# Attention and gated feed-forward on one core: keys of twelve tiles projected in four column groups, weight loads held back at transpositions, head reordered

## The chip, the cores and the metric

The kernel runs on one core of a Trainium2 chip. The metric is the device time of one execution in microseconds (us). The engines in the text are TensorE (PE, matrix products; PEld is its weight load), VectorE (DVE), ScalarE (ACT), GpSimd (POOL) and SyncE (SP, which only issues DMAs here). The core's memory has 128 partitions; products land in PSUM banks of 128 x 512 float32 values.

## What is computed

One pre-norm transformer block on x of 2048 rows and 1024 columns in bf16. The first half is attention with 32 query heads of 32 columns that share one key head and one value head. The second half is a gated feed-forward (FFN) of width 3584.

```python
q = (x @ wq).reshape(B, S, H, Dh).transpose(0, 2, 1, 3)
k = x @ wk
v = x @ wv
scores = einsum("bhqd,bkd->bhqk", q, k) * Dh ** -0.5
o = einsum("bhqk,bkd->bhqd", softmax(scores), v)      # then back to (B, S, H * Dh) @ wo
h = x + A(layernorm(x))
h2 = h + (sigmoid(n @ w_gate) * (n @ w_up)) @ w_down  # n = layernorm(h)
```

## The kernel before

**Tiles.** The 2048 rows are 16 tiles of 128. Two neighbouring tiles form a unit of the FFN, so there are eight units. Attention of a tile runs as four groups of eight heads over half of the keys each; a group is eight "bursts". A burst (`s_burst`) is four products of 32 x 512, one in each row group of the array, and fills four PSUM banks with scores of one key tile. ACT takes them in two exponentials of 128 x 1024 (`one_exp`, line 768). There are 512 bursts. The keys therefore have to stand four times over the partitions (`kT4`): the array's row group j reads keys from partitions 32j to 32j+31.

**Head.** Up to about burst 64 ("the head") the kernel normalizes x tile by tile (`ln1_stats`, `ln1_sub`, `ln1_mult`), transposes each normalized tile into `xnT`, and projects keys, values and queries from it. Tiles 0 and 1 are transposed by PE through PSUM banks of `S_ps` (`pe_transpose`, `pe_out`), the others by a DMA transposition on SP's queue (`transposed`, line 564). The key weights of 32 columns are copied four times side by side (`wk4`, 128 columns), so that `k_group` gives the four copies in one product per 128 rows of the contraction: eight products of 128 columns for each key tile. `v_group` and `q_tile` / `q_group` project values and queries. The groups of the head wait in a list `todo`, whose order is the string list `TODO`; `head_group` takes the first of it that is ready.

**Products by columns.** After a product with scores (four row groups) a change to another shape of the array costs PE time. A product for the FFN or the projections can also be cut into four column groups of 32 (`mm`, line 344, four instructions) so that no change of shape stands between it and the products of probabilities and values (`pv_group`, line 855), which use column groups too.

**Sums of probabilities.** For most groups DVE adds the probabilities in pairs (lines 805 and 817) and PE multiplies one sum with ones (line 902). For the groups marked `p` in `SUM_PLAN` PE multiplies all eight bursts with ones itself (line 917).

**After attention of a tile.** The output projection (`wo_group`), the second normalization (`stats2`, on DVE and POOL), and a DMA transposition on SP's queue (`transpose2`, `QT<-hn`). Then the unit's gate and up products (weights in halves of 512 KB that SP loads as slots come free), and its down products (`down_group`), whose weights `wd` (14 loads of 512 KB, `load_wd`, on POOL's queue) go into the places that x and the query weights held and stay there. The first down product waits for all 14. When only the first tile of a unit is ready, its gate and up products are done alone (`first_tile`), the other's come later.

**Order.** All instructions are emitted by a planner: a loop at the end of the kernel keeps an estimated clock for each engine and each DMA (`k_pe`, `k_dma`, the costs `T_EXP` and others) and decides, burst by burst, which group PE takes next. Strings steer it: `PV_PLAN` has a letter for each group of probabilities times values, `WO_PLAN` for each unit's output projection. `urgent(c)` puts a unit's output projection and normalization ahead when the unit before it is nearly through. The order on the chip is then fixed; only waits can stretch it.

**Start.** SP issues the left half of x tile 0, tiles 1 to 3, then three of the four parts of wq; ACT's queue issues the right half of tile 0, wk, the first part of wq, and wv. The first burst needs the queries of heads of q blocks 0 to 3, which come from the first two parts of wq.

Of the kernel before, what the change touches and what calls it, by code (L numbers as in the profile page):

```python
# [12 lines left out]
P = 128  # L13
# [55 lines left out]
class _Group:  # L69


    def __init__(self, items, evac, after=(), kind="f"):
        self.items = collections.deque(items)
        self.evac = evac
        self.after = after
        self.bank = None
        self.kind = kind
        self.room = 0.5
        self.first = False
# [5 lines left out]
def bass_sequential_preLN__grouped_kv_mqa__glu_gated_glu__prompt_kernel(  # L85
# [70 lines left out]
    with ExitStack() as es:  # L156
# [99 lines left out]
        def _(unused):  # L256
            sp, pe, act, dve, pool = nc.sync, nc.tensor, nc.scalar, nc.vector, nc.gpsimd

            def dma(q, dst, src, c, kb=256):
# [3 lines left out]
                k_dma[0] = begin + kb / 275.0  # L263
                c.at[c.n] = k_dma[0] + 2.2
# [60 lines left out]
            I_US, I_MAX = 4.0, 240  # L325
# [112 lines left out]
            mean_val, xc_val = {}, {}  # L438
            LOADS = {2: (4, 5), 3: (6, 7), 4: (8, 9), 5: (10, 11), 6: (12,), 7: (13,), 8: (14,), 9: (15,)}

            def ln1_stats(t, parts=(0, 1)):
# [5 lines left out]
                if parts[-1] == 0:  # L447
                    return
                need(dve, c_dve.inc(ins))
# [52 lines left out]
            def pe_transpose(t):  # L502

                need(pe, xn_val[t], ident_val)
                for dt in range(DT):
                    ins = pe.matmul(S_ps[:, 2 * t + dt // 4, dt % 4 * P:(dt % 4 + 1) * P], lhsT=xn(t)[:, dt * P:(dt + 1) * P],
# [9 lines left out]
            def pe_out(eng, t, h0, h1, *ticks):  # L516
                need(eng, *ticks)
                dst = xnT_tile(t)[:, 4 * h0:4 * h1, :]
                src = S_ps[:, 2 * t + h0:2 * t + h1, :].rearrange("p a (b q) -> p (a b) q", q=P)
# [41 lines left out]
            def transposed(eng, dst, src, slot, *ticks):  # L561
# [7 lines left out]
                c.at[c.n] = max(clk[0], k_dma[0] if eng is sp else 0.0) + 2.0  # L569
# [1041 lines left out]
```

## Time and profile before

| | |
|---|---|
| median of 3 runs | 1100.51 us (1100.1 to 1102.04) |
| the profiled execution | 1100.78 us |
| its span, first to last instruction | 1099.0 us |
| DVE busy | 895.4 us (81%) |
| ACT busy | 1003.7 us (91%) |
| POOL busy | 63.8 us (6%) |
| mean granted clock of PE | 0.997 |

Times inside the profile run from the first instruction. A row of a timeline has the start, the length, the engine, the line of the kernel, the operation, what it writes and reads, the shape and how many instructions were merged; in brackets the time for which the engine stood idle before it, and what ended that. A product's recorded length holds its way through the array, so that neighbours overlap; the distance between starts is what it costs PE. A row of a table by stretches has the stretch, its length, the busy time of each engine with the number of instructions, the granted clock, the share of DMA time and GB/s.

### The profile page before, as it was taken

What the parts mean: (1) busy time and instruction counts of PE and PEld (TensorE: products, weight loads), DVE (VectorE), ACT (ScalarE), POOL (GpSimd) and SP (SyncE); (2) the same over time, 40 slices, a digit from 0 to 9 for tenths busy, and PEclk for the clock granted to TensorE, in tenths of its full rate; (3) what the DMA queues carried; (4) which work ended last, traced back from release to release, by engine and by line L of the source; (5) the groups of instructions that cost most, each with busy time, mean ns of one, the idle gap of its engine ahead of it and who ended that gap; (6) DMA issues with size and microseconds to landing.
All of it is one profiled execution on the core that took longest, in us unless ns stands there. A gap on an engine that the chain in (4) does not pass through costs nothing.

```text
span 1099.0 us, 34241 instructions
## 1 busy us (share of the span) xinstructions
PE 1070.7 (97%) x15024; PEld 618.1 (56%) x15076; DVE 895.4 (81%) x1485; ACT 1003.7 (91%) x1145; POOL 63.8 (6%) x136
## 2 busy tenths in 40 slices
PE   8999979999999999999999999999999999999999
PEld 7443346643666346653666446653666447653884
DVE  7969878798988989798988988989988888798311
ACT  7999979999999999999999999999999999998110
POOL 3420010100000000000000000000000000000000
PEclk9999999999999999999999999999999999999999
DMA  8673246960976539791876619671495619662660
GB/s 194 139 157 134 64 111 193 270 150 21 236 204 189 135 92 249 196 214 31 212 206 187 153 31 260 192 190 38 129 244 157 147 35 258 191 186 57 162 161 20
DMA packets 320229, 170.12 MB, mean 155 GB/s; under 512 B 39376, under 2 KB 314064, under 8 KB 320080
## 3 DMA queue, kind: packets, MB, share of 16 engines
q1 hardware_dynamic: 314272, 157.70, 56.6%
q0 software_dynamic: 2544, 9.44, 2.7%
q8 instruction: 119, 1.95, 0.8%
q10 hardware_dynamic: 3264, 0.79, 0.4%
q14 instruction: 30, 0.25, 0.1%
HBM read 155.84 MB, written 4.19 MB: 146 GB/s over the span
## 4 chain that ended last, share of the span: by engine, by line
PE 79%; ACT 10%; DMA 4%; DVE 3%; issue 3%; POOL 1%; SPq 0%; ACTq 0%; DVEq 0%
PE X_ps L342 43%; PE X_ps L344 14%; PE S_ps L748 12%; PE X_ps L855 9%; ACT Pr L768 8%; DMA QT<-hn 2%; DMA wgu<-in_B_w_up_dram 1%; DMA zone<-in_A_wq_dram 1%; ACT QT L768 1%; PE X_ps L902 1%; ACT wo L768 1%; PE X_ps L917 0%; DVE pairs L805 0%; DMA zone<-hn 0%; POOL sd L424 0%
## 5 line engine op out<-in xcount | busy, mean ns | idle before, releaser
L768 ACT ACTIVATE Pr<-S_ps 128x1024 bf16<-128x1024 f32 x992 | 943.6, 1188 | 9.4 <-PE S_ps L748 8.7
L805 DVE TENSOR_TENSOR pairs<-Pr 128x1024 bf16<-128x1024 bf16 x470 | 320.3, 683 | 27.5 <-ACT Pr L768 27.1
L817 DVE TENSOR_TENSOR pairs<-pairs 128x1024 bf16<-128x1024 bf16 x408 | 281.4, 690 | 11.8
L748 PE MATMUL S_ps<-QT,kT 32*128 32x512 bf16 x2048 | 202.2, 385 | 4.3 <-ACT Pr L768 2.9
L342 PE MATMUL X_ps<-QT,wgu 128*128 128x128 bf16 (+1 forms) x2073 | 197.0, 245 | 2.4 <-DMA QT<-hn 1.2
L342 PEld LDWEIGHTS X_ps<-QT,wgu 128*128 128x128 bf16 x2073 | 153.8, 98 | 37.9 <-issue 22.6
L342 PE MATMUL X_ps<-QT 128*128 128x128 bf16 (+1 forms) x1484 | 142.5, 245 | 0.1
L748 PEld LDWEIGHTS S_ps<-QT,kT 32*128 32x128 bf16 x2048 | 51.5, 91 | 160.3 <-ACT Pr L768 145.8
L342 PE MATMUL X_ps<-zone,hact 128*128 128x512 bf16 (+2 forms) x599 | 137.0, 370 | 4.6 <-issue 4.0
L1172 ACT ACTIVATE gu<-X_ps 128x512 f32<-128x512 f32 x112 | 86.5, 773 | 48.4 <-PE X_ps L342 48.3
L1194 DVE SCALAR_TENSOR_TENSOR hact<-gu,X_ps 128x512 bf16<-128x512 f32 x112 | 76.6, 684 | 63.4 <-PE X_ps L342 52.6
L855 PE MATMUL X_ps<-Pr,V 128*32 128x512 bf16 x1984 | 128.0, 381 | 0.3 <-issue 0.3
L342 PEld LDWEIGHTS X_ps<-QT 128*128 128x128 bf16 x1484 | 110.4, 98 | 23.8 <-issue 14.5
L342 PEld LDWEIGHTS X_ps<-zone,hact 128*128 128x128 bf16 x636 | 55.0, 98 | 68.4 <-issue 16.1
L855 PEld LDWEIGHTS X_ps<-Pr,V 128*32 128x32 bf16 x1984 | 46.7, 96 | 52.5 <-issue 15.2
L344 PE MATMUL X_ps<-zone,hact 128*32 128x512 bf16 x1152 | 72.3, 380 | 0.0
L344 PE MATMUL X_ps<-QT,wgu 128*32 128x256 bf16 (+1 forms) x2076 | 63.6, 264 | 0.0
L344 PEld LDWEIGHTS X_ps<-QT,wgu 128*32 128x32 bf16 x2076 | 48.8, 97 | 12.7 <-issue 7.7
L413 POOL CAST mean<-mv 128x1 f32<-128x1 bf16 x28 | 7.3, 260 | 836.3 <-DVE mv L1064 808.7
L342 PE MATMUL X_ps<-wo,QT 128*128 128x512 bf16 x191 | 48.4, 380 | 1.4 <-issue 1.0
L342 PE MATMUL X_ps<-zone 128*128 128x128 bf16 (+3 forms) x442 | 45.0, 250 | 0.6 <-DMA zone<-in_A_wq_dram 0.5
L344 PEld LDWEIGHTS X_ps<-zone,hact 128*32 128x32 bf16 x1152 | 28.8, 96 | 29.3 <-issue 5.9
(99 smaller groups left out, 653.7 us busy)
## 6 DMA issues: line engine op xcount, KB each, us to landing
wgu<-in_B_w_gate_dram SPq DMA_DIRECT2D x75, 512.0 KB, 5.6
wgu<-in_B_w_up_dram SPq DMA_DIRECT2D x74, 512.0 KB, 5.2
QT<-in_B_w_up_dram SPq DMA_DIRECT2D x49, 512.0 KB, 5.3
QT<-in_B_w_gate_dram SPq DMA_DIRECT2D x48, 512.0 KB, 5.5
zone<-in_B_w_down_dram POOLq DMA_DIRECT2D x14, 512.0 KB, 5.4
hx<-in_A_x_dram SPq DMA_DIRECT2D x17, 256.0 KB, 2.8
out_dram<-hx SPq DMA_DIRECT2D x31, 128.0 KB, 1.7
Pr<-in_B_w_gate_dram SPq DMA_DIRECT2D x5, 512.0 KB, 7.0
```

Source lines behind the costliest of these rows:

```text
L342: return pe.matmul(out, lhsT=lhsT, rhs=rhs, start=start, stop=stop, skip_group_check=main[0])
L344: ins = pe.matmul(out[DH * j:DH * (j + 1)], lhsT=lhsT[:, DH * j:DH * (j + 1)], rhs=rhs, start=start, stop=stop, tile_position=(0, DH * j), ...
L413: return c_pool.inc(pool.tensor_copy(out=mean[:, i:i + 1], in_=mv[:, i:i + 1, 0]), 0.2)
L748: ins = pe.matmul(S_ps[:, ((2 * k + j // 2) % 3) * 2 + j % 2, :], lhsT=kT4[DH * j:DH * (j + 1), kt * P:(kt + 1) * P], rhs=QT[DH * j:DH * ( ...
L768: c_e.inc(act.activation(out=p_tile(k, n % 2), in_=S_ps[:, 2 * pr:2 * pr + 2, :].rearrange("p a (b q) -> p (a b) q", q=QC), func=ACTF.Exp, ...
L805: slot_use[x] = c_dve.inc(dve.tensor_tensor(out=dst(x), in0=p_tile(k - 1, hh), in1=p_tile(k, hh), op=ALU.add), T_ADD, 0.08)
L817: slot_use[x] = slot_use[y] = c_dve.inc(dve.tensor_tensor(out=pairs[:, x, :], in0=pairs[:, x, :], in1=pairs[:, y, :], op=ALU.add), T_ADD, ...
L855: ins = pe.matmul(bank[DH * j:DH * (j + 1), :], lhsT=V[:, kt, :], rhs=p_tile(kx, j // 2)[:, j % 2 * 2:j % 2 * 2 + 2, :], start=b == bs[0], ...
L902: ins = pe.matmul(bank[DH * j:DH * (j + 1), :], lhsT=ones[:], rhs=pairs[:, sum_wide[(g, j // 2)], j % 2 * 512:(j % 2 + 1) * 512], start=Tr ...
L1172: tanh_val[n] = c_act.inc(act.activation(out=slot, in_=bank, func=ACTF.Tanh, scale=0.5), T_TANH, 0.1)
L1194: gu_read[n] = c_dve.inc(dve.scalar_tensor_tensor(out=hact[:, 2 * fs[0]:2 * fs[0] + ft, r0:r0 + len(ts) * P], in0=slot.rearrange("p (a b) ...
```

## The change

Keys of tiles 0 to 3 are projected as before. Keys of tiles 4 to 15 come in three groups of four tiles: `kc_group` (C1 to C3) projects a tile in each column group with the 32 columns of `wk`, DVE copies the result to a staging place, and `kr_group` multiplies it with columns of the unit matrix, which spreads each tile's keys over the four partition groups; DVE copies that to `kT4`. The staging place is the old place of `wk4`. A C group waits until four tiles of `xnT` are there.

`load_wd` isn't issued while `turning()` holds: from the time at which a tile's attention is normalized until its transposition has landed. The down loads begin at burst 50 in place of 10, and all of them wait for the exponentials of the burst before.

At the start the second part of wq is issued ahead of x tiles 2 and 3, and x tiles 4 and 5 follow the third and fourth part; the keys and the first two query pairs of tile 0 are projected ahead of the transposition of tile 1, which now uses other banks; the first burst waits for tile 0 alone. The list `TODO` has another order.

Some PSUM evictions of the queries move between ACT and DVE (`T_PLAN`, `Q_PLAN`), `SUM_PLAN` marks one group more (group 4) for PE, `urgent` goes by the work left (`U_PLAN`), and the planner's strings, thresholds and costs have new values.

```diff
+    ROOM = 0.5
...
-    NEAR = 2
-    PV_PLAN = "BDaeeaaaAbbaaBbaAEeAababaAbBeAaaEAAaeDbdeaAbbbaEDabAAabaAaaabaAaacbcabDa"
-    WO_PLAN = "bbabaaaa"
+    U_PLAN = "65531610"
+    PV_PLAN = "aeaadddabaadbababaBbEdaaAaBbebdaaCdDdacaabAAdaaBaaCdDacdaaaaccbaaBbBaaaE"
+    WO_PLAN = "abbabaaa"
-    BANK_WAIT = 0
+    BANK_WAIT = 0.05
-    SUM_PLAN = "ppppdddp"
+    LN_RATE = 0.3
+    T_PLAN = "aaadddad"
+    H_ROOM = 0.5
+    Q_PLAN = "daddddddddddddddddadddddddddaddd"
+    SUM_PLAN = "pppppddp"
-    TODO = ["k1", "k0", "q1a", "q1b", "q0a", "q0d", "q0c", "q0b", "k2", "q1d", "k5", "k4", "ka", "v1", "v0", "k7",
-            "q1c", "v3", "v2", "k3", "k6", "kc", "kf", "kd", "kb", "ke", "v4", "v7", "v5", "k8", "v6", "Q2",
-            "k9"]
+    TODO = ["v7", "q1a", "k2", "q1b", "C1", "v1", "q1c", "v5", "v4", "k1", "C2", "v3", "Q2", "q0c", "q0d", "v2",
+            "v6", "C3", "v0", "q1d", "k3"]
-    WD_FROM, WD_GAP, WD_LATE = 10, 4, 6
-    K_ACT = 2
-    T_MM, T_FIX, T_SW, T_EXP, T_TANH, T_ADD = 0.0004167, 0.00267, 0.104, 0.91, 0.48, 0.61
+    WD_FROM, WD_GAP, WD_LATE = 50, 4, 14
+    K_ACT = 0
+    T_MM, T_FIX, T_SW, T_EXP, T_TANH, T_ADD = 0.0004167, 0.00267, 0.1, 0.907, 0.479, 0.61
...
-            for t in range(1, 4):
-                load_x(t)
+            load_x(1)
             wk_val = dma(act, wkr, A_wk.rearrange("(a p) j -> p a j", p=P), d_w[0], 64)
             wq_val[0] = dma(act, wq[:, 0, :, :], wqr[:, :, 0:256], d_w[2], 512)
+            load_wq(1, 256, 256)
+            for t in range(2, 4):
+                load_x(t)
             wv_val = dma(act, wv, A_wv.rearrange("(a p) j -> p a j", p=P), d_w[1], 64)
-            for i in range(1, 4):
+            for i in range(2, 4):
                 load_wq(i, 256 * i, 256)
+                load_x(i + 2)
...
-            I_US, I_MAX = 4.0, 240
+            I_US, I_MAX = 4.0, 210
...
-            LOADS = {2: (4, 5), 3: (6, 7), 4: (8, 9), 5: (10, 11), 6: (12,), 7: (13,), 8: (14,), 9: (15,)}
+            LOADS = {2: (6, 7), 3: (8,), 4: (9, 10), 5: (11,), 6: (12,), 7: (13,), 8: (14,), 9: (15,)}
...
+            def kc_group(i):
+                tiles = range(4 * i, 4 * i + 4)
+                items = []
+                for dt in range(DT):
+                    def f(bank, dt=dt):
+                        for j, t in enumerate(tiles):
+                            ins = pe.matmul(bank[DH * j:DH * (j + 1), 0:P], lhsT=wkr[:, dt, :],
+                                            rhs=xnT[:, t // TPQ, dt, t % TPQ * P:(t % TPQ + 1) * P], start=dt == 0,
+                                            stop=dt == DT - 1, tile_position=(0, DH * j), skip_group_check=True)
+                        return mm_done(ins, 144, dt == DT - 1)
+                    items.append((0.06, f))
...
+                    need(dve, tick)
+                    stage_val[i] = c_dve.inc(dve.tensor_copy(out=stage(i), in_=bank[:, 0:P]), 0.25, 0.08)
+                    for t in tiles:
+                        xnT_done(t // TPQ, tick)
+                    todo.insert(0, ("r", i))
...
+            def kr_group(i):
+                c0, items = 4 * i * P, []
+                for j in range(4):
+                    def f(bank, j=j):
+                        for r in range(4):
+                            ins = pe.matmul(bank[DH * r:DH * (r + 1), j * P:(j + 1) * P], lhsT=stage(0)[:, DH * j:DH * (j + 1)],
+                                            rhs=stage(i), start=True, stop=True, tile_position=(0, DH * r),
+                                            skip_group_check=True)
+                        return mm_done(ins, 144, j == 3)
+                    items.append((0.06, f))
...
+                    v = c_dve.inc(dve.tensor_copy(out=kT4[:, c0:c0 + 4 * P], in_=bank), 0.65, 0.08)
...
-                need(pe, (c_e, 2 * k - 1) if k > 0 else None, *s_ready(k), *(xnT_ready(0, 1) if k < 2 else ()))
+                need(pe, (c_e, 2 * k - 1) if k > 0 else None, *s_ready(k), *(xnT_ready(*range(k + 1)) if k < 2 else ()))
...
-                return not q_list and downs <= NEAR and downs < len(ffn_list) and unit_of(ffn_list[downs]) == c
+                if q_list:
+                    return False
+                left = 0.0
+                for x in ffn_list:
+                    if unit_of(x) == c:
+                        return left <= 3.0 * int(U_PLAN[c])
+                    left += {"p": 7.0, "l": 3.5, "g": 1.75, "u": 1.75, "d": 6.0}[x[0][0]]
+                return False
...
             ln1_stats(0)
+            ln1_sub(0)
             ln1_stats(1)
-            ln1_sub(0)
+            ln1_mult(0)
+            ln1_stats(1, ())
             ln1_sub(1)
-            ln1_mult(0)
...
             f0, f1 = pe_transpose(0)
+            xnT_val[0] = [pe_out(act, 0, 0, 1, f0), pe_out(dve, 0, 1, 2, f1)]
             ln1_mult(1)
-            xnT_val[0] = [pe_out(act, 0, 0, 1, f0), pe_out(dve, 0, 1, 2, f1)]
+            run_group(k_group([0], True))
+            run_group(q_tile(0, [0, 1], True))
+            run_group(q_tile(0, [2, 3], True))
             f0, f1 = pe_transpose(1)
...
-                return len(xn_val) >= min(NT, (k[0] // 4 if k[0] < NHB else k[0] - NHB + BPG) + LN_LEAD)
+                return len(xn_val) >= min(NT, int(LN_LEAD + LN_RATE * k[0]))
...
+            def turning():
+                t = len(hnT_val)
+                return t < NT and (t, NQ // 2 - 1) in ot_val or t and when(hnT_val[t - 1]) > k_pe[0]
...
-                if wd_free and wo_val[0] and k[0] >= wd_at[0] and when(*wd_free[0][1]) <= k_pe[0]:
+                if wd_free and wo_val[0] and k[0] >= wd_at[0] and when(*wd_free[0][1]) <= k_pe[0] and not turning():
                     load_wd()
```

More of the change, by code (lines that the diff above doesn't have):

```diff
@@ L518, in pe_out @@
                 dst = xnT_tile(t)[:, 4 * h0:4 * h1, :]
[L519 removed]
+                src = S_ps[:, 4 * t + h0:4 * t + h1, :].rearrange("p a (b q) -> p (a b) q", q=P)
                 if eng is act:
@@ new lines, in kr_group, with evac @@
+            def kr_group(i):
[8 more added lines that the diff above has]
+                    items.append((0.06, f))
+                def evac(bank, tick):
+                    need(dve, tick)
+                    v = c_dve.inc(dve.tensor_copy(out=kT4[:, c0:c0 + 4 * P], in_=bank), 0.65, 0.08)
+                    for t in range(4 * i, 4 * i + 4):
+                        k_val[t] = v
+                        wk_done(tick)
+                    return v
+                return _Group(items, evac, [same_val[0], stage_val[i]], "pv")
@@ L1426, in head_group @@
                         ok = q_can(*x[1:], now)
+                    elif x[0] == "r":
+                        ok = when(stage_val[x[1]], same_val[0]) <= now
+                    elif x[0] == "C":
+                        tiles = range(4 * x[1], 4 * x[1] + 4)
+                        ok = len(k_val) >= 4 and all(t in xnT_val for t in tiles) and when(*xnT_ready(*tiles)) <= now
                     else:
@@ L1484, in _ @@
                 can_s = kk < NB and pv_done[0] >= ring_need(kk - 1 if late else kk) and (
-                    s_ready(kk) is not None and when(*s_ready(kk)) <= k_pe[0])
+                    kk >= NHB + 5 * BPG or s_ready(kk) is not None and when(*s_ready(kk)) <= k_pe[0])
                 hold = (busy(pv[0]) and plan_of(pv_next[0] - 1) in "deDE" and pe_mode[0] == "pv" and
```

56 lines of the change are left out of this document (39 added, 17 removed).

## The prediction

> **What bounds the kernel now.** I read the page first, then tables by stretches, the chain that ended last, and timelines of the places that these point to.
>
> ```profile
> span 1099.0 us, 34241 instructions
> PE 1070.7 (97%) x15024; PEld 618.1 (56%) x15076; DVE 895.4 (81%) x1485; ACT 1003.7 (91%) x1145; POOL 63.8 (6%) x136
> ACT  7999979999999999999999999999999999998110
> PE 79%; ACT 10%; DMA 4%; DVE 3%; issue 3%; POOL 1%; SPq 0%; ACTq 0%; DVEq 0%
> ```
>
> PE holds 79% of the chain. ACT is full until slice 37 and then nearly idle: the exponentials are over, and PE works off what is left.
>
> ```profile
> 30.00:60.00 30.00, 27.42 (x561) 13.96 (x561) 26.88 (x63) 30.00 (x34) 12.84 (x31) 1.00 0.63 123
> 140.00:160.00 20.00, 15.29 (x245) 9.27 (x242) 18.96 (x33) 18.07 (x21) 4.08 (x7) 0.99 0.51 120
> 160.00:180.00 20.00, 16.96 (x301) 12.35 (x302) 12.25 (x20) 14.98 (x18) 0.72 (x1) 0.84 0.49 125
> 800.00:900.00 100.00, 99.03 (x1296) 54.28 (x1296) 86.24 (x138) 100.00 (x116) 1.93 (x4) 1.00 0.58 148
> 900.00:1000.00 100.00, 98.53 (x1538) 60.00 (x1539) 87.15 (x142) 99.31 (x115) 3.51 (x7) 1.00 0.71 184
> ```
>
> In the table by stretches PE and ACT are both full from 800 to 1000 us. So the time is the sum of PE's work and of PE's gaps. A us less of either pulls the end forward by a us, as long as PE has products at hand. The large gap lies between 140 and 180 us: 7.7 us without PE work, and a granted clock of 0.84 in the second half.
>
> **Term 1: the down loads leave the transposition of tile 1.**
>
> ```profile
> 151.54 1.49 POOL L260 DMA_DIRECT2D zone<-in_B_w_down_dram  x2
> 152.19 1.24 SPq L564 DMA_TRANSPOSE QT<-hn  x1
> 162.41 1.36 PE L342 MATMUL X_ps<-QT,zone 128*128 128x128 bf16 x11 [6.64 <-DMA QT<-hn]
> 164.35 1.94 ACT L768 ACTIVATE Pr<-S_ps 128x1024 bf16<-128x1024 f32 x2 [6.28 <-PE S_ps L748]
> 162.00:166.00 4.00, 3.59 (x32) 2.96 (x33) 0.59 (x1) 1.65 (x2) 0.00 (x0) 0.50 0.00 0
> QT<-hn SPq DMA_TRANSPOSE x1, 10.2
> QT<-hn SPq DMA_TRANSPOSE x1, 4.4
> 131.84 1.24 SPq L564 DMA_TRANSPOSE QT<-hn  x1
> QT<-hn SPq DMA_TRANSPOSE x1, 6.7
> 236.45 4.08 SPq L564 DMA_TRANSPOSE QT<-hn  x1
> ```
>
> Two down loads of 512 KB are issued at 151.5 us, the transposition at 152.19, and it lands 10.2 us later. PE stands 6.64 us, and then works four us at half clock: 3.6 us of work at 0.50 lose 1.8 us. ACT stands 6.28 us of the same time. The transposition of tile 0 (131.84) took 4.4 us, that of tile 2 (236.45) took 6.7 us; no down load is issued beside either. The change forbids the loads from a tile's normalized attention to the landing. At 4.4 us the landing comes at 156.6 in place of 162.4: the gap shrinks by 5.8 us to 0.8, and the 1.8 us go too. That is 7.6 us. With 6.7 us the gap keeps 3.1 us; what the clock does after 3.1 us no row shows (the row shows it after 6.64), so the gain is 3.5 to 5.3 us. I take 7.6: as in the row of 4.4, SP has only loads of x close by. The upper bound is 8.4, the whole gap and its slow clock.
>
> The Trainium skill ("TensorE: Matmul & The Clock Gate", section "HAM oscillation — how this bites in real kernels") asks that PE have no idle gap above about 3.4 us, since one makes it start again at half clock. The trace agrees with its 6.64 us gap and the clock of 0.50. By that rule a gap of 3.1 us costs only itself, and the gain would be 5.3 us.
>
> **Term 2: keys in four column groups.**
>
> ```profile
> 45.34 0.63 PE L344 MATMUL X_ps<-zone 128*32 128x128 bf16 x32
> 45.78 0.40 PE L917 MATMUL X_ps<-Pr,ones 128*32 128x512 bf16 x4
> 134.84 1.48 PE L917 MATMUL X_ps<-Pr,ones 128*32 128x512 bf16 x24
> 67.22 4.89 DMA zone<-hn
> ```
>
> The row at 45.34 is one key tile by columns: eight sets of four products, and the next work starts 0.44 us later, 55 ns a set. Twelve tiles take 96 sets. The change takes 3 x 8 for the projection and 3 x 4 for the spreading, of the same shape: 36. Sixty sets less are 3.3 us. The four streams now read different rows; in the row at 134.84, where each set of four ones products reads four different slices of probabilities, a set costs (1.48 - 0.39) / 5 = 0.218 us for 512 columns, a fourth of which is again 55 ns.
>
> The same part marks group 4 for PE in the sums. It then takes eight sets with ones in place of one: seven more at 0.218 us are 1.5 us of PE. DVE loses eight adds and six merges at about 0.69 us, but DVE isn't the bound. Net, 1.8 us off PE. It counts while queries are still being projected when the FFN begins; they are:
>
> ```profile
> 138.32 0.82 PE L342 MATMUL X_ps<-zone 128*128 128x512 bf16 x3
> 138.98 0.94 PE L342 MATMUL X_ps<-QT,zone 128*128 128x128 bf16 x14
> ```
>
> The last query product ends and the first gate product starts without a gap, so what the head saves starts the FFN earlier. DVE's twelve key evictions become three small and three wide ones, which is free. The keys now come in batches: the batch of tiles 12 to 15 needs the transposition that lands at 67.22 + 4.89 = 72.1 us, then some 2 us of projecting, copying, spreading and copying. Burst 36 uses it first, at 12.5 + 36 x 1.83 = 78 us (both from term 3). Covered by 4 us; if normalization slips by more, every us of it stops ACT and PE alike.
>
> **Term 3: the start.**
>
> ```profile
> 2.97 8.91 DMA zone<-in_A_wq_dram
> 8.22 0.58 ACT L521 ACTIVATE zone<-S_ps 128x512 bf16<-128x512 f32 x1
> 9.13 0.68 DVE L522 CAST zone<-S_ps 128x512 bf16<-128x512 f32 x1
> 11.50 0.38 ACT L642 ACTIVATE QT<-X_ps 128x256 bf16<-128x256 f32 x1 [0.62 <-PE X_ps L342]
> 11.92 1.34 PEld L342 LDWEIGHTS X_ps<-zone 128*128 128x128 bf16 x24 [0.64 <-DMA zone<-in_A_wq_dram]
> 13.63 0.39 PE L748 MATMUL S_ps<-QT,kT 32*128 32x512 bf16 x4
> 28.85 14.63 ACT Pr L768 x16
> DMA packets 6929, 3.28 MB, mean 234 GB/s; under 512 B 2223, under 2 KB 6544, under 8 KB 6928
> ```
>
> The row at 28.85, from the chain, gives 14.63 / 8 = 1.83 us for a burst of two exponentials. The second part of wq is issued behind four loads of x and lands at 11.9; the first burst follows at 13.63. The change puts it ahead of two loads of 256 KB: at the 234 GB/s of the first 14 us that is 2.2 us, landing at 9.7. Then another chain ends last. Tile 0 is evicted from PSUM at 9.8; eight key sets and 32 query products of 55 ns follow (2.2 us), then the eviction of 0.38: the burst starts at 12.5, a gain of 1.1 us. Bounds: 0, if the first part of wq on ACT's queue, now beside the second, lands at 11.9 instead, and 1.7, the wait up to 11.92 against the eviction at 9.8 less 0.4 for the keys. I take 1.1. x tiles 2 and 3 land 2.2 us later; their keys are used only from 28 us, so that is free.
>
> **What I cost at nothing.** ACT takes over five query evictions (0.38 us each for three of 256 columns, 0.58 each for two of 512, as in the rows at 11.50 and 8.22) and gives up one of 128 columns (0.28, as 256 columns lie 0.2 apart): 2.0 us more. It lies beside PE's backlog, since PE still works for 80 us when ACT is through; the second rival has the price without that cover. The new order of the groups removes no product and no burst. PE's gaps per 100 us between 300 and 1000 us range from 0.97 to 1.47 (the rows of 800 and 900), under many different orders; over eight such stretches that is 4 us, either way. The gaps of the head between 30 and 60 us are 2.6 us; earlier loads of x and a freer DVE could close them or leave them: bounds 0 and a gain of 2.6, taken as 0, since in that stretch ACT is full too.
>
> **The sum.** 1100.78 (span 1099.0 and 1.8 around it) - 7.6 - 1.8 - 1.1 = 1090.3 for a profiled execution like this one; that execution lies 0.3 above the median of 1100.51, so 1090.0.
>
> **Rivals.** *The down weights come late; slower than before.*
>
> ```profile
> 118.23 0.69 DVE L960 TENSOR_TENSOR QT<-hact,ols 128x512 bf16<-128x512 f32 x1
> 140.81 0.69 DVE L960 TENSOR_TENSOR QT<-hact,ols 128x512 bf16<-128x512 f32 x1
> 177.68 0.72 POOL L260 DMA_DIRECT2D zone<-in_B_w_down_dram  x1 [24.65 <-ACT Pr L768]
> 185.99 0.72 POOL L260 DMA_DIRECT2D zone<-in_B_w_down_dram  x1 [7.59 <-ACT Pr L768]
> 219.02 0.69 DVE L960 TENSOR_TENSOR QT<-olp,ols 128x512 bf16<-128x512 f32 x1
> 234.13 1.03 PE L342 MATMUL X_ps<-zone,hact 128*128 128x512 bf16 x4
> zone<-in_B_w_down_dram POOLq DMA_DIRECT2D x14, 512.0 KB, 5.4
> ```
>
> Loads start at burst 50 (104 us) and stop at 118, when tile 0 is normalized: four, two bursts apart. One fits between the landing for tile 0 (136) and the end of tile 1's attention (141). From 155 on they come 8.3 us apart, as in the two rows: seven until tile 2 is normalized, at 219.0 less 8.7 = 210. Two are left until its transposition lands, at 236.45 + 6.7 - 8.7 = 234, and the last lands at 234 + 8.3 + 5.4 = 248. The first down product could start at 234.1 - 8.7 = 225. FFN products stand 23 us; they are about two thirds of PE's time in a burst of 1.83 us (scores and values take a set of 0.22 each, and with the changes of shape I count a third for them), so PE loses 15 us: 1105. It beats the gain from a stand of 16 us on. Against it: with the FFN standing, tile 2's projection would run at once, the block would end some 6 us sooner, and a load more may fit before 210.
>
> The Trainium skill ("DMA: Bandwidth & Descriptors", section "Issuing engines are not separate DMA queues") says that transfers started by any engine run on the same 16 DMA engines and interleave. By that, three loads moved from before 152 us to later would meet SP's gate and up loads there, which speaks for this rival.
>
> *ACT sets the end.* ACT gains 1.1 at the start and 5.5 of its 6.28 us stand, and loses 2.0; if PE finds nothing to do in place of what it saves, the end moves with ACT by 4.6 us: 1096. For it: 100% in the row of 800. Against: PE's tail of 80 us holds work that could come sooner.
>
> *The transposition stays at 6.7 us*, beside SP's own weight loads: 2.3 to 4.1 us of term 1 are lost, 1092 to 1094. Part of the change then doesn't do what it says.
>
> *The head's gaps close too*: 1087.
>
> **Chances.** Forecast 0.52 (its own range 1084 to 1095, by the bounds above); late down weights 0.18; ACT 0.13; slow transposition 0.12; closed gaps 0.05. The range of 1083 to 1100 leaves out the late down weights and the lowest ends. Faster by over 0.2% (about 2 us, what a measurement can tell from no change) 0.81; within it 0.03, slower 0.16, both nearly all from the first rival.
>
> **What would show it.** Right: a first burst near 12.5 us; a transposition of tile 1 under 5 us, no PE gap above 1 us before 170 us, and no stretch under full clock; 96 key products of 32 columns for projecting and 48 for spreading. Wrong: PE gaps around 220 to 245 us with a down load landing just before the first down product; a wait of scores for keys at 43, 71 or 78 us; a tail after the last exponential that is as long as before.

## The result and the profile after

| | before | after |
|---|---|---|
| median of 6 runs | 1100.3 us (1098.21 to 1102.04) | 1095.48 us (1095.27 to 1096.63) |
| the profiled execution | 1100.78 us, span 1099.0 | 1095.49 us, span 1093.7 |
| ratio, 95% interval | | 0.996 (0.9947 to 0.9972) |

The change makes the kernel faster by 4.8 us, where 10.5 were forecast.

The page after, its span and busy times; then a table by stretches (stretch, length, busy time of each engine, granted clock, DMA share, GB/s); then the transposition of tile 1, with the time from issue to landing:

```profile
span 1093.7 us, 32972 instructions
PE 1076.3 (98%) x14429; PEld 612.2 (56%) x14429; DVE 886.8 (81%) x1462; ACT 1005.0 (92%) x1149; POOL 63.0 (6%) x136
...
30.00:60.00 30.00, 26.68 (x517) 12.66 (x513) 25.26 (x57) 29.38 (x33) 9.76 (x24) 1.00 0.50 103
140.00:160.00 20.00, 19.95 (x323) 12.86 (x316) 17.88 (x31) 20.00 (x24) 3.14 (x5) 1.00 0.46 127
160.00:180.00 20.00, 19.98 (x355) 13.89 (x353) 16.69 (x27) 20.00 (x26) 1.44 (x2) 1.00 0.90 253
180.00:200.00 20.00, 15.94 (x170) 9.57 (x168) 17.03 (x28) 20.00 (x25) 2.17 (x3) 1.00 0.80 223
200.00:204.00 4.00, 4.00 (x44) 1.31 (x44) 2.42 (x4) 2.67 (x4) 0.00 (x0) 0.57 0.40 145
...
QT<-hn SPq DMA_TRANSPOSE x1, 3.0
```

PE's 7.7 us without work at 140 to 180 us are gone, and the transposition takes 3.0 us in place of 10.2. There are new losses: 30 to 60 us has lost 0.7 us of PE's work and 0.6 of ACT's, and from 180 to 200 us PE stands for 4 us, after which its clock is halved for a while.

Where the time went is seen best if the execution is cut at four score bursts. The numbers are the distances between the first score products of bursts 0, 64, 80 and 511 in the trace, and the span's end:

| us | before | after | forecast | measured |
|---|---|---|---|---|
| start to burst 0 | 13.6 | 13.6 | -1.1 | 0.0 |
| burst 0 to 64, the head | 117.9 | 122.8 | -1.8 | **+4.9** |
| burst 64 to 80, with the transposition of tile 1 | 39.2 | 31.1 | -7.6 | **-8.1** |
| burst 80 to 511 | 840.2 | 840.5 | 0 | +0.3 |
| burst 511 to the end | 88.1 | 85.7 | 0 | -2.4 |

The forecast has its -1.8 in the head because the prediction says that "what the head saves starts the FFN earlier". A second profile of the changed kernel (the last run below) gives 124.0, 31.1, 840.5 and 85.7 us, and a first burst at 14.78 us: behind burst 64 the stretches repeat, the start and the head vary by about a us.

Next the groups of ACT from 14 to 131 us, before and then after: what it writes and reads, the count, the busy time and the mean ns of one, and the idle time before them.

```profile
L768 ACT ACTIVATE Pr<-S_ps 128x1024 bf16<-128x1024 f32 x95 | 88.4, 1127 | 0.1
L768 ACT ACTIVATE wo<-S_ps 128x1024 bf16<-128x1024 f32 x16 | 15.3, 1091 | 0.3 <-PE S_ps L748 0.3
L768 ACT ACTIVATE QT<-S_ps 128x1024 bf16<-128x1024 f32 x16 | 15.1, 1075 | 0.3 <-PE S_ps L748 0.3
```

```profile
L834 ACT ACTIVATE Pr<-S_ps 128x1024 bf16<-128x1024 f32 x90 | 84.0, 1082 | 1.6 <-PE S_ps L814 1.6
L834 ACT ACTIVATE QT<-S_ps 128x1024 bf16<-128x1024 f32 x16 | 15.6, 1048 | 1.3 <-PE S_ps L814 1.3
L834 ACT ACTIVATE wo<-S_ps 128x1024 bf16<-128x1024 f32 x16 | 15.4, 1109 | 0.0
L728 ACT ACTIVATE QT<-X_ps 128x512 bf16<-128x512 f32 (+1 forms) x3 | 1.6, 545 | 0.1
L703 ACT ACTIVATE QT<-X_ps 128x256 bf16<-128x256 f32 x2 | 0.8, 380 | 0.0
```

Before, ACT makes 127 exponentials in these 117 us and is idle for 0.7 us: it is the engine that paces the head. After, it makes 122. It has 2.4 us of query evictions to do and is idle for 3.0 us. Its idle pieces above 0.2 us, on its own timeline:

```profile
16.64 1.94 ACT L834 ACTIVATE QT<-S_ps 128x1024 bf16<-128x1024 f32 x2 [0.29 <-PE S_ps L814]
18.92 1.02 ACT L834 ACTIVATE QT<-S_ps 128x1024 bf16<-128x1024 f32 x1 [0.34 <-PE S_ps L814]
57.00 1.94 ACT L834 ACTIVATE QT<-S_ps 128x1024 bf16<-128x1024 f32 x2 [0.62 <-PE S_ps L814]
82.59 8.39 ACT L834 ACTIVATE Pr<-S_ps 128x1024 bf16<-128x1024 f32 x9 [1.64 <-PE S_ps L814]
```

What lies behind them, and behind the start, on PE's timeline:

```profile
9.47 0.61 PE L350 MATMUL X_ps<-zone 128*128 128x128 bf16 x8 [1.39 <-ACT zone L532]
11.10 1.96 PE L350 MATMUL X_ps<-zone 128*128 128x128 bf16 x32 [1.02 <-DMA zone<-in_A_wq_dram]
...
36.93 0.63 PE L636 MATMUL X_ps<-zone 128*32 128x128 bf16 x32 [1.28 <-DMA zone<-hn]
56.01 0.63 PE L636 MATMUL X_ps<-zone 128*32 128x128 bf16 x32 [0.75 <-issue]
82.16 0.40 PE L814 MATMUL S_ps<-QT,kT 32*128 32x512 bf16 x4 [1.35 <-issue]
```

Line 636 is the projection of a key batch: C1 at 36.93 waits for a transposition, C2 at 56.01 stands too, and ACT's piece of 0.62 us follows it. The gap at 82.16, by far the largest on ACT, has no releaser that the profile shows. At the start wq still ends the wait for the queries, at 11.1 us.

### The profile page after: what moved, and what is told of

Same layout as the page of the kernel before. It is cut to its first block, busy times and chain, and to the rows that moved or that the text cites. A ratio compares the mean times of both kernels' runs of the same rounds, so it can differ in the third digit from the quotient of the medians.

```text
span 1093.7 us, 32972 instructions
## 1 busy us (share of the span) xinstructions
PE 1076.3 (98%) x14429; PEld 612.2 (56%) x14429; DVE 886.8 (81%) x1462; ACT 1005.0 (92%) x1149; POOL 63.0 (6%) x136
## 3 DMA queue, kind: packets, MB, share of 16 engines
q8 instruction: 113, 1.85, 0.7%
## 5 line engine op out<-in xcount | busy, mean ns | idle before, releaser
L871 DVE TENSOR_TENSOR pairs<-Pr 128x1024 bf16<-128x1024 bf16 x462 | 314.7, 683 | 26.1 <-ACT Pr L834 25.4
L883 DVE TENSOR_TENSOR pairs<-pairs 128x1024 bf16<-128x1024 bf16 x402 | 277.5, 690 | 12.2
L350 PE MATMUL X_ps<-QT,wgu 128*128 128x256 bf16 (+1 forms) x2145 | 210.2, 247 | 0.1
L350 PEld LDWEIGHTS X_ps<-QT,wgu 128*128 128x128 bf16 x2145 | 161.9, 98 | 39.9 <-issue 24.8
L350 PE MATMUL X_ps<-zone,hact 128*128 128x512 bf16 (+2 forms) x678 | 155.6, 372 | 0.0
L352 PE MATMUL X_ps<-zone,hact 128*32 128x512 bf16 x984 | 62.5, 380 | 0.0
L352 PE MATMUL X_ps<-QT,wgu 128*32 128x256 bf16 (+1 forms) x1724 | 53.9, 264 | 0.1
L350 PE MATMUL X_ps<-wo,QT 128*128 128x512 bf16 x216 | 53.6, 380 | 0.0
L352 PEld LDWEIGHTS X_ps<-QT,wgu 128*32 128x32 bf16 x1724 | 40.4, 97 | 11.9 <-issue 6.8
L1302 DVE SCALAR_TENSOR_TENSOR hx<-X_ps,hx 128x512 bf16<-128x512 f32 (+2 forms) x33 | 22.2, 671 | 25.5 <-PE X_ps L350 23.9
```

The costliest lines, as they stand in the source:

```text
L350: return pe.matmul(out, lhsT=lhsT, rhs=rhs, start=start, stop=stop, skip_group_check=main[0])
L352: ins = pe.matmul(out[DH * j:DH * (j + 1)], lhsT=lhsT[:, DH * j:DH * (j + 1)], rhs=rhs, start=start, stop=stop, tile_position=(0, DH * j), ...
L871: slot_use[x] = c_dve.inc(dve.tensor_tensor(out=dst(x), in0=p_tile(k - 1, hh), in1=p_tile(k, hh), op=ALU.add), T_ADD, 0.08)
L883: slot_use[x] = slot_use[y] = c_dve.inc(dve.tensor_tensor(out=pairs[:, x, :], in0=pairs[:, x, :], in1=pairs[:, y, :], op=ALU.add), T_ADD, ...
L1302: v = c_dve.inc(dve.scalar_tensor_tensor(out=hv, in0=bank[:, 0:n], scalar=0.5, in1=hv, op0=ALU.mult, op1=ALU.add), 0.03 + n * 0.00113, 0.08)
```

## The experiments

### Mixtures of the two kernels

Four kernels take one part of the change alone or undo one. The planner decides everything anew in them. (The theories A and B of these four texts are not those of the later ones: one gives the gain to the new order of work, the other to the rule for the down loads.)

The first is the kernel before with the rule for the down loads; the second the changed kernel without it:

```diff
-    WD_FROM, WD_GAP, WD_LATE = 10, 4, 6
+    WD_FROM, WD_GAP, WD_LATE = 50, 4, 14
...
-                if wd_free and wo_val[0] and k[0] >= wd_at[0] and when(*wd_free[0][1]) <= k_pe[0]:
+                if wd_free and wo_val[0] and k[0] >= wd_at[0] and when(*wd_free[0][1]) <= k_pe[0] and not turning():
```

> The kernel before with the new policy for the down loads alone (none before burst 50, none from a tile's normalized attention to the landing of its transposition, all paced by the exponentials). Theory A: the stand of 6.6 us at the transposition of tile 1 and its half clock go, but the gate and up products of unit 0 are fed through four weight places, so PE stands again before the first down product at 234 us; 1098.5 to 1100 us. Theory B: the 8 us stay in hand, and what is missing from the changed kernel's gain is lost in its head (burst 64 comes 4.8 us later than before); 1092 to 1094 us.

> The changed kernel with the old policy for the down loads. Theory A: 1096 to 1098 us, since the policy is worth little. Theory B: 1102 to 1104 us, the stand of about 8 us comes back in full.

The third is the changed kernel with `PV_PLAN`, `WO_PLAN`, `urgent`, `BANK_WAIT` and `I_MAX` of before; the fourth is the kernel before with those of the changed one.

> The changed kernel with the old order strings and thresholds (PV_PLAN, WO_PLAN, urgent, BANK_WAIT, I_MAX). Theory A: the gain of the change comes from the order after 240 us, some 3.5 us; 1098 to 1100 us. Theory B: the order is worth nothing that can be measured; 1095 to 1096.5 us.

> The kernel before with the new order strings and thresholds alone. Theory A: 1096 to 1098 us. Theory B: 1099.5 to 1101 us.

Measured, beside 1098.9 us (1097.24 to 1100.25) of the kernel before in the same comparison, with the stretches of the table above:

| kernel | median us | ratio (95%) | head | 64 to 80 | 80 to 511 | after burst 511 |
|---|---|---|---|---|---|---|
| before + rule for down loads | 1107.62 | 1.0082 (1.0067 to 1.0097) | 117.7 | 31.7 | 844.8 | 98.8 |
| changed - rule for down loads | 1115.3 | 1.015 (1.0135 to 1.0165) | 123.4 | 35.4 | 840.8 | 99.8 |
| changed, old order | 1111.85 | 1.012 (1.0105 to 1.0135) | 122.8 | 31.9 | 846.7 | 95.5 |
| before, new order | 1107.24 | 1.0074 (1.0057 to 1.0091) | 119.6 | 37.4 | 841.6 | 96.0 |

Both theories missed: every mixture is slower than both kernels. Most of the loss is not in the part exchanged but behind burst 511, in all four. In the first, bursts 64 to 80 take 31.7 us, nearly as with the whole change (31.1), and burst 80 comes 8.4 us earlier than before; but 98.8 us are left after burst 511 in place of 88.1. PE had no products at hand in the middle and has them all still before it at the end. The table by stretches and the first down product of that kernel:

```profile
220.00:260.00 40.00, 30.91 (x255) 12.00 (x255) 32.74 (x53) 36.51 (x41) 2.34 (x5) 0.83 0.34 76
...
241.25 0.63 PE L342 MATMUL X_ps<-zone,hact 128*128 128x512 bf16 x1 [1.85 <-DMA zone<-in_B_w_down_dram]
```

PE is without work for nine of 40 us. For 6.5 of them it waits for ACT between bursts, with no FFN product at hand, and the last 1.85 us are ended by a down load: this is the rival "the down weights come late" of the prediction. It does happen with this rule, in another order of work; the changed kernel's order avoids it. The order strings fit one kernel, and a part exchanged under them tells of the misfit, not of the part. So the rest was done with the order held fixed: the planner's clocks are updated as in the original, and only what is issued differs.

### The price of the transposition, by itself

In the kernel before, the seventh and eighth down loads wait on POOL until tile 1's transposition has landed. In the changed kernel, the other way round, its fifth and sixth are put off to the place behind POOL's 1/sigma of tile 1, so that they run beside the transposition.

```diff
+                if wd_next[0] in (7, 8):
+                    pool.wait_ge(d_t[1].sem, d_t[1].n + (0 if 1 in hnT_val else 16))
                 wd_val[0] = dma(pool, wd[:, 2 * i:2 * i + 2, :],
```

```diff
+                if wd_next[0] in (5, 6):
...
+                    deferred.append((wd[:, 2 * i:2 * i + 2, :], src))
+                    return
...
                             ln2_pow[t] = ln_rstd(idx, st2_val[t])
+                        while t == 1 and deferred:
+                            pool.dma_start(*deferred.pop(0)).then_inc(d_wd.sem, 16)
```

> The kernel before with every instruction in its order on every engine; only the two loads of the down weight that it issues at 151.5 us now wait on POOL for the landing of tile 1's transposition. So nothing is decided anew, and the price of the 10.2 us transposition is seen by itself. Both theories: the transposition takes about 3 us, PE's wait of 6.6 us for it at 155 to 168 us is gone, burst 80 starts near 163 us instead of 170.7. Theory K (what the stand cost is kept, and what the changed kernel lacks it lost by its own order of work): everything behind comes 7 to 8 us earlier and stays so; 1092 to 1094 us, ratio 0.993 to 0.9955, gate and up products done by 220 us up by 3 us or more against 42.4. Theory R (the first unit's products cannot run faster than their weights come through four places, so an earlier start is lost again by 240 us whatever the order): new waits of PE for weights between 170 and 240 us, burst 96 or 112 at most 3 us earlier than before; 1096.5 to 1099.5 us, ratio 0.997 to 1.0.

> The changed kernel with every instruction of PE, ACT, DVE and SP in its order; only two loads of the down weight (those issued at 137.6 and 145.2 us) are put off to the place that two have in the kernel before, behind POOL's 1/sigma of tile 1 and so beside tile 1's transposition. Both theories: the transposition takes 7 us or more instead of 3.0, and PE waits for it. Theory K: the changed kernel loses what the stand cost, 5 to 8 us, and keeps the loss to the end: 1100.5 to 1103.5 us, ratio to the kernel before 1.001 to 1.004. Theory R: the stand of 4 us and the half clock that the changed kernel has between 180 and 204 us shrink by as much as its products start later; 1095.5 to 1098.5 us, ratio 0.996 to 0.9985.

Measured beside 1099.05 us of before: the waiting loads 1092.67 us, ratio 0.9948 (0.9933 to 0.9964); the loads beside the transposition 1103.72 us, ratio 1.0046 (1.003 to 1.0062). Theory K holds in both directions, with both times inside or 0.2 us outside its ranges, and R falls. The first lines are of the waiting loads (stretches, then the transposition of tile 1), the second of the loads put beside it (its transposition, then PE's wait in the list of waits: us in total, times, longest):

```profile
140.00:160.00 20.00, 18.81 (x303) 12.24 (x302) 19.00 (x33) 20.00 (x24) 3.53 (x6) 1.00 0.43 134
160.00:180.00 20.00, 19.37 (x326) 12.95 (x327) 18.12 (x30) 20.00 (x24) 1.44 (x2) 1.00 0.77 213
...
QT<-hn SPq DMA_TRANSPOSE x1, 3.1
```

```profile
QT<-hn SPq DMA_TRANSPOSE x1, 6.2
...
PE X_ps L350 <- DMA QT<-hn: 3.3, 1, 3.3
```

Bursts 64 to 80 take 31.7 us with the waiting loads (39.2 before), and nothing of the 7.5 us is given back: 839.6 us follow to burst 511 and 88.3 to the end, as before. Two waits on POOL do alone what the whole change does, and more. One number of K missed: gate and up products done by 220 us are 43.7 us' worth against 42.4, at 0.417 ns a column, a lead of 1.3 us where 3 or more were expected. That costs nothing here, since by 240 us they are done in both. In the reverse the profiled execution has a transposition of 6.2 us only, where 7 or more were expected, and bursts 64 to 80 take 35.5 us against 31.1. At 1099.53 us it is the fastest of six; the others take 1102.59 to 1105.38 us. How long a transposition beside two loads lasts varies (6.2, 6.6, 9.9 and 10.2 us in four kernels that have it).

### What ACT's evictions and PE's saved sets are worth in the head

The same five query evictions that the change moved are done by the other engine, with the order of PE, POOL and SP kept: by DVE in the changed kernel, by ACT in the kernel of the waiting loads. In a third kernel the keys of tiles 4 to 15 take three contraction steps of eight, in the order of the waiting loads; its keys are incomplete sums.

```diff
+            def as_planned(eng, planned, at, lat, tick, ins_of, *more):
+                k_ = CLK[id(planned)]
+                k_[0] = max(k_[0], when(tick, *more)) + at
...
+                ins_of().then_inc(c.sem, 1)
...
+                    if (q, c0) in ((1, 256), (2, 1024), (4, 1536)):
+                        v = as_planned(act, dve, 0.12 + n * 0.00104, 0.08, tick,
+                                       lambda: act.activation(out=out, in_=src, func=ACTF.Copy),
```

```diff
+                def step(bank, dt):
+                    if tiles[0] >= 4 and 2 <= dt < DT - 1:
+                        return mm_done(None, n, False)
```

> The changed kernel with PE, POOL and SP in the same order; only the five query evictions that it had given to ACT are done by DVE, at the same place of the order. Theory A (ACT sets the end: it has hardly an idle us from the first burst to the last, and what PE saves is worth nothing until then): ACT gets rid of about 2.2 us, all of it by burst 64, and everything behind comes as much earlier: 2.0 to 2.4 us less than the changed kernel, 1093.0 to 1093.6 us, ratio to the kernel before 0.9935 to 0.995. Theory P (as predicted: these evictions lie beside PE's backlog and cost nothing): no difference or a loss of up to 0.5 us by DVE, 1095.3 to 1096 us.

> The kernel of the two waiting loads (before's order, 1092.7 us), with PE, POOL and SP in the same order; the same five query evictions go from DVE to ACT. Theory A: 2.0 to 2.4 us more, 1094.6 to 1095.2 us, ratio 0.9965 to 0.998 against 0.9948. Theory P: 1092.3 to 1093.0 us.

> The kernel of the two waiting loads with every instruction in its order, but the keys of tiles 4 to 15 are projected with three of the eight contraction steps: 60 sets less on PE, as many as the change saves, without its batches and without a new order. It leaves out part of the keys' sums. Theory A: PE only waits longer for ACT, the time is within 0.7 us of 1092.7 us. Theory P: 3.3 us less, 1089.0 to 1090.0 us, ratio 0.991 to 0.992.

| kernel | median us | ratio (95%) | head | after burst 511 |
|---|---|---|---|---|
| changed, five evictions on DVE | 1096.25 | 0.9976 (0.9967 to 0.9985) | 123.3 | 85.7 |
| waiting loads, five evictions on ACT | 1095.01 | 0.9969 (0.9958 to 0.998) | 120.0 | 88.1 |
| waiting loads, sixty key sets less | 1091.78 | 0.9939 (0.9925 to 0.9952) | 118.7 | 88.0 |

*The evictions on ACT* cost 2.1 us, all in the head (117.9 to 120.0), and the median rises by 2.3 us. Theory A has it. ACT's groups from 14 to 131 us in that kernel:

```profile
L794 ACT ACTIVATE Pr<-S_ps 128x1024 bf16<-128x1024 f32 x94 | 87.6, 1117 | 0.1
L794 ACT ACTIVATE wo<-S_ps 128x1024 bf16<-128x1024 f32 x16 | 15.6, 1090 | 0.3 <-PE S_ps L774 0.3
L794 ACT ACTIVATE QT<-S_ps 128x1024 bf16<-128x1024 f32 x16 | 15.2, 1065 | 0.3 <-PE S_ps L774 0.3
L684 ACT ACTIVATE QT<-X_ps 128x512 bf16<-128x512 f32 (+1 forms) x3 | 1.7, 560 | 0.1
L655 ACT ACTIVATE QT<-X_ps 128x256 bf16<-128x256 f32 x2 | 0.8, 412 | 0.0
```

The idle time is 0.8 us, where the waiting loads have 0.7, and two exponentials fewer are done than the 128 of the waiting loads in the same stretch. ACT is full, so what it is given comes on top.

*Sixty sets less* do not shorten the head: 118.7 us against 117.9. The stretches from 14 to 131 us, of the waiting loads and then of that kernel:

```profile
14.00:131.00 117.00, 113.45 (x1825) 53.28 (x1822) 101.02 (x204) 116.62 (x128) 26.45 (x59) 1.00 0.52 128
```

```profile
14.00:131.00 117.00, 111.21 (x1640) 49.93 (x1638) 99.99 (x203) 115.71 (x127) 26.04 (x59) 0.99 0.53 128
...
36.54 0.43 PE L751 MATMUL S_ps<-QT,kT 32*128 32x512 bf16 x4 [1.17 <-ACT Pr L771]
36.90 1.05 PE L858 MATMUL X_ps<-QT,V 128*32 128x512 bf16 x8
```

PE is busy 2.2 us less and waits longer for ACT. The 0.8 us more belong to this execution, the slowest of five: PE is granted half the clock from 36.8 to 40.2 us, behind the wait of 1.17 us (the eight products at 36.90 take 1.05 us, which take 0.6 us elsewhere), and from burst 36 to burst 64 both kernels take 51.3 us. The median is 0.9 us under that of the waiting loads, 0.2 us outside the range of theory A, and the intervals overlap; the 3.3 us of theory P are excluded. What the run can't show is what another order would make of PE's free time, since here the order is fixed.

*The evictions on DVE* missed. In the changed kernel's own order the head stays at 123.3 us (122.8 with the evictions on ACT), and the ratio is not lower than the changed kernel's, so theory A fails as a statement about that kernel: ACT is not the only one that paces it. Three of ACT's idle pieces in that run, on its timeline, and PE's waits for the batches:

```profile
23.44 7.44 ACT L853 ACTIVATE wo<-S_ps 128x1024 bf16<-128x1024 f32 x8 [0.60 <-PE S_ps L833]
38.95 9.29 ACT L853 ACTIVATE Pr<-S_ps 128x1024 bf16<-128x1024 f32 x10 [0.69 <-PE S_ps L833]
58.70 1.94 ACT L853 ACTIVATE QT<-S_ps 128x1024 bf16<-128x1024 f32 x2 [1.29 <-PE S_ps L833]
```

```profile
37.33 1.04 PE L636 MATMUL X_ps<-zone 128*32 128x128 bf16 x32 [1.36 <-DMA zone<-hn]
57.71 0.63 PE L636 MATMUL X_ps<-zone 128*32 128x128 bf16 x32 [1.44 <-issue]
```

What ACT is spared it now idles: 5.0 us from 14 to 131 us against 3.0. Of these, 1.9 us lie in the first bursts, up to 23.4 us, 0.7 and 1.3 us behind C1 and C2, and 0.8 us at 94 and 124 us; only the gap at 82 us is smaller, 0.3 us. The scores behind a batch come late, whoever evicts the queries. Two things add to it that were not tried alone: DVE, which now makes the five evictions, also normalizes the tiles for the batches, and PE has half the clock from 37.2 to 40.6 us in this execution, so that the 32 products of C1 take 1.04 us in place of 0.63.

### The load of wo, and both kernels side by side

In the gap of 1.35 us that ends at 82.16 us, 0.3 us after its start, POOL issues the 2 MB load of wo. One kernel holds that load back by eight bursts; it has the evictions on DVE too.

```diff
-                    wo_val[0] = dma(pool, wo[:], A_wo.rearrange("(q p) n -> p q n", p=P), d_wo, 2048)
...
+                if wo_from[0] is not None and k[0] >= wo_from[0]:
+                    pool.wait_ge(c_e.sem, 2 * k[0] - 2)
+                    pool.dma_start(wo[:], A_wo.rearrange("(q p) n -> p q n", p=P)).then_inc(d_wo.sem, 16)
```

> As the changed kernel with the five evictions on DVE, and besides the 2 MB load of wo, which POOL issues at 81.1 us, waits for eight more bursts. It tells where the changed kernel's gap of 1.35 us on PE and 1.64 us on ACT at 81 us comes from. If from this load: no such gap, burst 36 another 1.3 to 1.6 us earlier, 1.3 to 1.6 us less than the kernel with the evictions alone. If not: the same gap at the same burst, and the same time as that kernel within 0.4 us.

1096.46 us, ratio 0.9984 (0.9974 to 0.9994), head 123.8 us. A gap of 0.83 us on PE and 1.12 us on ACT stays at the same burst although wo isn't being loaded, and the kernel with the evictions alone, which loads wo as the changed kernel does, has none there. So the load of wo isn't its cause.

Last, the kernel of the waiting loads and the changed kernel in one comparison:

> The kernel of the two waiting loads once more, beside the changed kernel on the same chip, since the two were timed in different comparisons (0.9948 and 0.9960) with intervals that overlap. If the rest of the change loses time on the whole: this kernel is 2 to 4 us faster than the changed one, 1092 to 1093.5 us. If the rest is worth nothing either way: the two are within 1 us of each other.

> The changed kernel, unaltered, in the same comparison: 1095 to 1096.5 us if the rest of the change loses time on the whole, within 1 us of the kernel of the two waiting loads if it is worth nothing. Its profile also shows how far the start and the gap at 81 us vary from one execution to the next: the first burst at 13.5 us and the gap of 1.35 us come back if they belong to the order of work, and move by 0.5 us or more if they don't.

Beside 1099.06 us of before: 1093.35 us, ratio 0.9945 (0.9931 to 0.9959), against 1095.31 us, ratio 0.9967 (0.9955 to 0.9979). Their medians differ by 2.0 us, at the lower end of what was expected. The intervals just overlap, but the five executions of the one (1092.6 to 1093.55 us) all lie below the nine of the other (1094.37 to 1097.83). The best kernel of the study that computes everything is the one before with two loads that wait; the rest of the change is worth nothing to it on the whole, and more likely costs 2 us. Part of these 2 us goes with the clock. The mean granted clock is 1.0 in all five executions of the waiting loads. In the changed kernel it is 0.998 in two, which take 1094.4 and 1094.7 us, 0.997 in four (1095.2 to 1097.0) and 0.995 in three (1097.0 to 1097.8).

## Why the prediction was wrong

**Term 1 was right**, in mechanism, place and size: -7.6 us forecast, -8.1 in the profile, -7.5 in bursts 64 to 80 with the waiting loads alone (-6.4 in the median). The transposition landed even sooner than in the row of 4.4 us that it was sized by. The new stand of PE at 180 to 200 us did not take the gain back: bursts 80 to 511 last about as long as in the kernel of the waiting loads, 840.5 against 839.6 us. ACT is full through the stand, and the half clock behind it costs some 1.5 us (last section).

**The step that failed** is the one on the head: "It counts while queries are still being projected when the FFN begins", for the key sets, and "It lies beside PE's backlog", for ACT's five evictions. PE has that backlog only from the first gate product on, at 138 us. Until then its products are few, its order has no spare ones to pull forward, and ACT's exponentials set the pace. So 1.8 us saved on PE there are not 1.8 us; in the row from 30 to 60 us, 30.00 busy for ACT beside 27.42 for PE had said so. And 2.0 us more for ACT, costed at nothing, are 2.1 us by the run that adds them alone, in the order of before. The sentence "a us less of either pulls the end forward" was read off the stretch of 800 us and carried to one with other limits. The rival "ACT sets the end", at 1096 us, had the right price of the evictions and comes within 0.5 us of the result. That is in part luck: it had expected a shorter start to help, which did not come, and neither the idle time of ACT nor a gain in the tail.

**The batches' cover was sized for the wrong one.** The prediction checks burst 36, which needs the batch of tiles 12 to 15, and finds 4 us. C1 and C2, which it did not check, are the ones that stand: 1.28 and 0.75 us of PE's waits, of which 0.6 us reach ACT in this profile (0.5 behind C1 and 0.8 behind C2 in the second one). The wait of C1 seems to have a second price. PE has half the clock for 3.4 us from 37 to 38.5 us on in six of the seven profiled executions with the batches, and in two of the seven without them; the profile after, on which the table rests, is the one with batches that is spared.

So the 4.9 us of the head are, on ACT's timeline, 2.4 us of evictions and 2.3 us more of idle time: 1.6 at the gap at 82 us, which the prediction couldn't know of, 0.6 behind C2 and 0.6 at the first bursts, less the 0.6 that ACT idled before. This is an account of one execution and not of causes. In the order of before the evictions alone cost 2.1 us, but in the changed order the head keeps its length without them; and none of the idle pieces was tried alone. What sets the length of the changed head stays open to that extent.

**Term 3 was mis-sized**: -1.1 us forecast, nothing gained. The first burst starts at 12.93 to 13.63 us in seven profiled executions with the start of before (mean 13.15) and at 13.33 to 15.07 in seven with the new one (mean 13.94). The two latest, 14.78 and 15.07, have half the clock from about 11 us on; the other five have a mean of 13.55. The term let the eviction of tile 0 end the chain at 9.8 us, with wq there at 9.7. But wq landed at 11.1; the part on ACT's queue is the late one, as the lower bound of 0 supposed; the part on SP's queue, which was put ahead, landed at 8.9. ACT also makes its second subtraction ahead of its half of tile 0's eviction, and PE stands 1.39 us for that, but the keys are done before wq is there.

**The tail** was forecast unchanged and is 2.4 us shorter. The products that PE issues behind the last burst, at 0.417 ns a column, are 80.9 us in place of 83.0. The total of PE's products falls by 1.7 us, as term 2 has it (1.8). So PE's saving is not lost, it only can't be had in the head: the new order brings it, or a better packing, to the end. Which of the two was not tried.

**The slower rival** did not come: the first down product starts at 234.1 us before and at 235.1 after. The first mixture shows that it was a real danger.

## What to carry to other kernels

Cost an edit in the stretch in which it acts: an engine that has a backlog over the whole kernel may have none there, and then what it saves is idle time and what its neighbour takes on is time. When an order of work has been fitted to a kernel, hold it fixed to price a part; mixtures under a fitted order came out 8 to 16 us above the kernel before here. And where a stall has one cause in sight, try the smallest edit that removes it: two waits on one queue beat the whole change.

## What the runs showed of the hardware

**Half clock without a long gap.** The changed kernel is granted half the clock for 3.4 us from 200.2 us on, after stands of at most 1.17 us. The stretches of 2 us around it, and then those of the kernel with the evictions on DVE, which has the same stands and keeps the full clock:

```profile
196.00:198.00 2.00, 1.11 (x12) 0.56 (x10) 1.89 (x3) 2.00 (x4) 0.72 (x1) 1.00 1.16 289
198.00:200.00 2.00, 0.83 (x10) 0.39 (x7) 0.26 (x1) 2.00 (x3) 0.00 (x0) 1.00 0.96 250
200.00:202.00 2.00, 2.00 (x24) 0.81 (x24) 1.93 (x4) 2.00 (x3) 0.00 (x0) 0.54 0.76 273
```

```profile
196.00:198.00 2.00, 1.11 (x12) 0.62 (x10) 1.93 (x4) 2.00 (x4) 0.66 (x1) 1.00 1.22 291
198.00:200.00 2.00, 0.91 (x10) 0.51 (x6) 0.23 (x1) 2.00 (x4) 0.06 (x1) 1.00 1.00 261
200.00:202.00 2.00, 1.93 (x32) 0.76 (x32) 1.91 (x3) 2.00 (x4) 0.00 (x0) 1.00 0.86 313
```

PE is about half busy for 4 us in both, and one is slowed and the other not. It costs some 1.5 to 2 us: bursts 80 to 511 take 840.5 us with it, and 838.9, 838.5 and 838.4 in three kernels with this order that keep the full clock there. The Trainium skill ("TensorE: Matmul & The Clock Gate", section "What's actually happening") says that the gate watches PE's activity in a free-running window of about 3.4 us; the length of the slow stretch agrees, and such a window would explain why the same stands are punished in one execution and not in another.

The traces bear it out. Between 7 and 1000 us every slow stretch of the fourteen profiles lasts 3.41 us or a multiple of it, and several in one execution lie on one grid of such steps. In the twenty steps of full clock that come just before a slow stretch, PE's products, as recorded, cover 0.0 to 2.1 us of the 3.41; no step of full clock with less than 1.7 us is followed by another, and between 1.7 and 2.1 us both occur. Here the step before the slow stretch, from 196.7 us, has 1.55 us; in the kernel with the evictions on DVE the grid lies otherwise, and the step from 197.6 us has 2.14. So the clock goes by the share of PE's work in a step, and the rule of an idle gap above 3.4 us, weighed in the prediction, is not the whole of it: no gap here is that long, and stands of 3.3 us (the loads put beside the transposition) and 2.9 us (the fourth mixture) came with half the clock too. That answers what the prediction left open for a gap of 3.1 us.

**A gap at an instruction fetch.** In both profiles of the changed kernel PE's gap at 82 us starts when a 16 KB transfer of the instruction queue ends (80.6 us in the first), with the DMA engines full. Where that transfer ended more than 1 us ahead of the same place in PE's order, with the evictions on DVE, there is no gap. In the five profiles that have the gap its end comes 1.3 to 1.5 us after the transfer's end. That PE waits for its own instructions there fits all of them, but no run was made to show it.
